# Two units instead of three in the first gated sweep, scores of two heads in turn into four banks, one normalising product per pair

## The chip, the cores and the metric

The kernel runs on one core of a Trainium2 chip. The metric is the device time of one execution in microseconds. The engines are TensorE (PE, with its weight loads PEld), VectorE (DVE), ScalarE (ACT), GpSimd (POOL) and SyncE (SP), whose queue starts nearly all DMA transfers.

## What is computed

```python
# attention, batch 2, 8 heads, 768 positions, head size 64; n_global = 8, n_local = 96
scores = q @ k.T / sqrt(64) - slope[h] * dist      # kept: first n_global keys, last n_local keys
a = softmax(scores); x = a @ v                     # x: 1536 rows of 512
# gated block, d_ff = 1536
xn = x / rms(x) * rms_g
y = (silu(xn @ w_gate) * (xn @ w_val)) @ w_out
# top-1 of 8 experts, 512 -> 1024 -> 512
out[mask_e] = gate_w[mask_e] * (relu(y[mask_e] @ w1[e]) @ w2[e])
```

## The kernel before

**Attention.** The 1536 rows are six stages of two tiles of 128 rows. For each stage the kernel goes through four pairs of heads, and a unit is one tile of rows of one pair: 6 x 4 x 2 = 48 units, numbered from 0. `scores` (L511) multiplies queries and keys of the two heads of a unit into two PSUM tiles `sp`; DVE adds the table of distances and takes the row's least value (L557, into `pr` and `mx`); ACT takes the exponential (L561). `turn` (L569) transposes the probabilities on PE (`pp`, L572), and ACT copies them to `ptS` (L580). `values` (L585) multiplies them by the values (`xp`, L601), and after the pair's second tile DVE takes the reciprocal of the sums (L608, L609) and writes the normalised rows into `duo` (L611), one product for each of the two tiles. A unit's turn is issued two units behind its scores, its values three more behind that.

The first eight pairs (units 0 to 15, `is_raw`, L203) multiply queries and keys as they are, in full fp32: head 0 lies on partitions 0 to 63, head 1 on 64 to 127, and each product contracts over 64 rows of the array (L533 in the first two tiles of a batch; later L537 for the 32 global keys and L538 for the others). The pairs after that split queries and keys into a high and a low fp32r part (ACT L486 and L498, DVE L499, POOL L489) and contract over all 128 rows (L550). All scores take their banks from the tag `s`, which has two. In units 0 to 15 `warm` (L176) issues two products of zeros behind a unit's scores, into banks of the tag `mm`, which has three.

**The gated block.** When a stage's rows are done, `tail` (L381) normalises them (ACT L387, DVE L393), transposes (L400) and splits them into `xn` (ACT L403, DVE L404). The 12 slices of d_ff (m = 0 to 11, called gated units here) are done in sweeps: a sweep takes a few gated units for all six stages, so that the weights in SBUF serve six times. `moe_block` (L762) is one stage of one sweep: 24 products of 256 columns per gated unit (`pg`, L769), tanh and the gating (ACT L777, DVE L778 and L782, ACT L786, POOL L787), and 6 output products of 512 columns per gated unit (`po`, L806), accumulated over the sweep's units. Sweep 0 has units 0 to 2, sweep 1 units 3 and 4, sweep 2 units 5 and 6, the last 7 to 11. Sweep 0 is issued between the attention's units, as far as a credit of 0.5 per unit allows (loop at L1163); the other sweeps and what is left follow the attention.

**The weights** come as float64. `prep_steps` (L361) gives three steps per gated unit (gate, value, output). A step loads 512 KB through one of three buffers `raw` (L322) and converts it in `convert64`: ACT L334, four DVE operations (L337, L340, L343, L346), ACT L353, and L354 for the low part, on POOL during the attention and on DVE behind it (`pin["sweep"]`). `PREPS` says at which unit the next step of sweep 0's weights is issued; those of later sweeps are issued between the blocks of the sweep ahead.

**What sets the order.** Each engine runs its instructions in the order in which they stand on it. That order is not the written one: the framework places instructions by its own estimate of when they are ready, written order giving the priority, so that work written later can stand ahead. Where the table `PREPS` or the split into sweeps changes, the places of many instructions change.

Of the kernel before, what the change touches and what calls it, by code (L numbers as in the profile page):

```python
# [45 lines left out]
def kernel(  # L46
# [23 lines left out]
    M0 = [3] * NSTAGE  # L70
    M1 = 7
    PM = [[0, 1, 2], [3, 4, 5, 6], [7, 8, 9], [10, 11]]
# [5 lines left out]
    PREPS = [2, 4, 6, 7, 11, 12, 20, 28, 36]  # L78
# [98 lines left out]
    def warm(n, after=None):  # L177
        for _ in range(n):
            w = psum.tile([P, 512], F32, tag="mm", bufs=NMM, name="warm")
            i = nc.tensor.matmul(  # L180
                out=w.rearrange("p (a n) -> p a n", a=4), lhsT=wz, rhs=wz.unsqueeze(1).to_broadcast([P, 4, P]),
                start=True, stop=True,
            )
            if after is not None:
                behind(i, after)

# [103 lines left out]
    def body(is_fast):  # L290
# [70 lines left out]
        def prep_steps(ms, pool, nslot):  # L361

            steps = []
            for m in ms:
                def gv(i, w, m=m):
                    if i == 0:
                        weights[m, 0] = pool.tile([P, 2, 2, KD, P], F32R, tag="gv", bufs=nslot, name=f"gv{m}")
# [4 lines left out]
                def ow(m=m):  # L372
                    t = weights[m, 1] = pool.tile([P, 2, DM], F32R, tag="ow", bufs=nslot, name=f"ow{m}")
# [3 lines left out]
                steps += [lambda gv=gv: gv(0, w_gate), lambda gv=gv: gv(1, w_val), ow]  # L377
            return steps
# [31 lines left out]
        def fast_attention(pool):  # L410
# [102 lines left out]
            def scores(g, t):  # L513
# [4 lines left out]
                else:  # L518
                    sp = [ps("s", NS, "sp") for _ in range(2)]
# [7 lines left out]
                if raw_:  # L527
                    kn, kgr_ = kt
                    for j in range(2):
                        r = slice(D * j, D * (j + 1))  # L530
                        lq = qt[r, t * P:(t + 1) * P]
                        if t0 == 0:
                            mm = nc.tensor.matmul(  # L533
                                out=sp[j][:, 0:n], lhsT=lq, rhs=kn[r, 0:n], start=True, stop=True
                            )
                        else:
                            nc.tensor.matmul(out=sp[j][:, 0:GW], lhsT=lq, rhs=kgr_[r, hp, :], start=True, stop=True)  # L537
                            mm = nc.tensor.matmul(  # L538
                                out=sp[j][:, GW:n], lhsT=lq, rhs=kn[r, t * P + GW:(t + 2) * P], start=True, stop=True
                            )  # L540
# [12 lines left out]
                un = units.index((g, t))  # L553
                if un < WARMU:
                    warm(WARM2[un % len(WARM2)], mm)
# [29 lines left out]
            def values(g, t, ptf, nb):  # L585
# [19 lines left out]
                if t == nt - 1:  # L605
# [4 lines left out]
                    for tt in range(nt):  # L610
                        nc.vector.tensor_tensor(  # L611
                            out=part[STARTS[st] + tt][:, hp * P:(hp + 1) * P].rearrange("p (j d) -> p j d", j=2),
                            in0=xp[:, tt * VW + 1:tt * VW + 1 + P].rearrange("p (j d) -> p j d", j=2),
                            in1=rc[:, tt].unsqueeze(2).to_broadcast([P, 2, D]), op=ALU.mult,
                        )
# [539 lines left out]
        preps = prep_steps(PM[0], wp, 3)  # L1155
# [9 lines left out]
        while True:  # L1165
# [9 lines left out]
            while preps and nun > PREPS[9 - len(preps)]:  # L1175
                preps.pop(0)()
            credit += MOE_RATE
            while True:
                if moe is None and ready:
                    st = ready.pop(0)  # L1180
                    moe = moe_block(0, range(M0[st]), st, mpool, False)
# [14 lines left out]
        nx = prep_steps(PM[1], ea, 4)  # L1196
# [14 lines left out]
        for st in ready:  # L1211
            run(moe_block(0, range(M0[st]), st, mpool, False))
        drain(f() for f in nx)
        for lo, hi, ms, pool, nslot, every in ((3, 5, PM[2], wp, 3, 4), (5, M1, PM[3], ea, 4, 5)):
            nx = prep_steps(ms, pool, nslot)
# [164 lines left out]
```

## Time and profile before

| | us |
|---|---|
| median of 3 runs | 655.6 (655.58 to 659.03) |
| the profiled execution | 655.69 |
| its span, first to last instruction | 654.0 |
| PE busy | 628.9 (96%) |
| DVE busy | 446.2 (68%) |
| ACT busy | 320.3 (49%) |
| POOL busy | 208.7 (32%) |

Times in the trace count from the span's start. The scores of unit 0 come at 8.5 us, the last product of the attention's values at 170 us; behind that stand the gated sweeps and the experts. A matmul's row in a timeline lasts until its result is in PSUM, so the next one starts ahead of its end, and what one costs PE is read from start to start.

### The profile page before, as it was taken

What the parts mean: (1) busy time and instruction counts of PE and PEld (TensorE: products, weight loads), DVE (VectorE), ACT (ScalarE), POOL (GpSimd) and SP (SyncE); (2) the same over time, 40 slices, a digit from 0 to 9 for tenths busy, and PEclk for the clock granted to TensorE, in tenths of its full rate; (3) what the DMA queues carried; (4) which work ended last, traced back from release to release, by engine and by line L of the source; (5) the groups of instructions that cost most, each with busy time, mean ns of one, the idle gap of its engine ahead of it and who ended that gap; (6) DMA issues with size and microseconds to landing.
All of it is one profiled execution on the core that took longest, in us unless ns stands there. A gap on an engine that the chain in (4) does not pass through costs nothing. (4 is left out here: it accounts for less than half of the span.)

```text
span 654.0 us, 11691 instructions
## 1 busy us (share of the span) xinstructions
PE 628.9 (96%) x4280; PEld 562.3 (86%) x4281; DVE 446.2 (68%) x1098; ACT 320.3 (49%) x624; POOL 208.7 (32%) x275
## 2 busy tenths in 40 slices
PE   9998998899999999999999999999999999999992
PEld 4667887899999999999999999997888899899891
DVE  5765888976599988676359998944667464664410
ACT  3666798777555533334622221333656564654420
POOL 4415758663122212111222532461610221011010
PEclk9999899899999999999999999999999999999997
DMA  7536466551044532131311010442978667454000
GB/s 228 158 90 201 127 174 181 157 149 39 1 130 130 161 98 72 59 98 65 129 65 65 2 65 34 122 138 82 301 261 261 206 217 253 168 189 140 17 13 30
DMA packets 56567, 82.98 MB, mean 127 GB/s; under 512 B 7983, under 2 KB 38703, under 8 KB 56496
## 3 DMA queue, kind: packets, MB, share of 16 engines
q1 hardware_dynamic: 53552, 74.75, 36.9%
q0 software_dynamic: 2944, 7.35, 3.4%
q8 instruction: 37, 0.61, 0.4%
q14 instruction: 34, 0.28, 0.1%
HBM read 75.75 MB, written 7.39 MB: 127 GB/s over the span
## 5 line engine op out<-in xcount | busy, mean ns | idle before, releaser
L769 PE MATMUL pg<-xn,gv 128*128 128x256 f32 x1728 | 228.2, 285 | 1.2 <-DVE th L778 1.2
L769 PEld LDWEIGHTS pg<-xn,gv 128*128 128x128 f32 x1728 | 220.2, 192 | 8.2 <-DVE th L778 1.5
L787 POOL TENSOR_TENSOR hid<-hf,hid 128x256 fp32r<-128x256 f32 x72 | 61.4, 855 | 174.6 <-ACT hid L786 174.5
L806 PE MATMUL po<-ow,hid 128*128 128x512 f32 x432 | 113.9, 394 | 0.0
L1017 PE MATMUL py<-ew,eh 128*128 128x512 f32 x384 | 91.2, 395 | 0.9 <-DVE eh L1084 0.5
L1017 PEld LDWEIGHTS py<-ew,eh 128*128 128x128 f32 x384 | 71.3, 188 | 17.7 <-DVE eh L1084 0.9
L806 PEld LDWEIGHTS po<-ow,hid 128*128 128x128 f32 x432 | 75.5, 189 | 11.7 <-POOL hid L787 0.3
L1039 PE MATMUL ph<-xs,ew 128*128 128x256 f32 x672 | 83.1, 283 | 0.0
L1039 PEld LDWEIGHTS ph<-xs,ew 128*128 128x128 f32 x672 | 81.6, 191 | 0.7
L786 ACT ACTIVATE hid<-hf 128x256 fp32r<-128x256 f32 x72 | 29.9, 417 | 83.7 <-DVE hf L782 81.9
L1024 POOL DMA_INDIRECT out_dram<-yo,tk x16 | 16.5, 1034 | 139.1 <-ACT yo L1023 107.7
L838 DVE CUSTOM_DVE_ANT_0 jk<-duo,rgb 128x512 bf16<-128x512 f32 x64 | 54.3, 849 | 0.5
L561 ACT ACTIVATE pr<-pr,mx 128x256 f32<-128x256 f32 (+1 forms) x96 | 45.1, 484 | 14.0 <-DVE mx L557 13.2
L957 DVE TENSOR_TENSOR ew<-rawe,ew 128x1024 fp32r<-128x1024 f32 (+1 forms) x36 | 40.8, 1134 | 12.9 <-ACT ew L953 12.9
L1048 DVE SCALAR_TENSOR_TENSOR eh<-ph,eh 128x256 fp32r<-128x256 f32 x56 | 23.1, 423 | 37.5 <-ACT eh L1047 35.5
L777 ACT ACTIVATE th<-pg 128x256 f32<-128x256 f32 x72 | 27.2, 379 | 39.8 <-PE pg L769 37.3
L957 DVE TENSOR_TENSOR ew<-duo,ew 128x1024 fp32r<-128x1024 f32 x28 | 34.1, 1224 | 17.9 <-ACT ew L953 16.8
L953 ACT ACTIVATE ew<-rawe 128x1024 fp32r<-128x1024 f32 x36 | 38.0, 1059 | 10.2 <-PE pg L769 4.6
L778 DVE SCALAR_TENSOR_TENSOR th<-th,pg 128x256 f32<-128x256 f32 x72 | 29.7, 415 | 16.4 <-ACT th L777 15.4
L1047 ACT ACTIVATE eh<-ph 128x256 fp32r<-128x256 f32 x56 | 21.2, 384 | 39.2 <-PE ph L1039 38.1
L953 ACT ACTIVATE ew<-duo 128x1024 fp32r<-128x1024 f32 x28 | 29.4, 1059 | 19.4 <-PE py L1017 19.4
L815 DVE TENSOR_TENSOR duo<-duo,po 128x512 f32<-128x512 f32 x36 | 23.4, 684 | 18.7 <-PE po L806 18.6
(178 smaller groups left out, 935.8 us busy)
## 6 DMA issues: line engine op xcount, KB each, us to landing
rawe<-in_moe_w_dram SPq DMA_DIRECT2D x36, 512.0 KB, 5.0
duo<-in_moe_w_dram SPq DMA_DIRECT2D x28, 512.0 KB, 5.4
raw<-in_moe_w_gate_dram SPq DMA_DIRECT2D x12, 512.0 KB, 3.8
raw<-in_moe_w_val_dram SPq DMA_DIRECT2D x12, 512.0 KB, 5.6
raw<-in_moe_w_out_dram SPq DMA_DIRECT2D x12, 512.0 KB, 3.4
kn<-in_k_dram SPq DMA_DIRECT2D x28, 192.0 KB, 3.3
qn<-in_q_dram SPq DMA_DIRECT2D x36, 128.0 KB, 2.9
vn<-in_v_dram SPq DMA_DIRECT2D x16, 192.0 KB, 2.6
```

Source lines behind the costliest of these rows:

```text
L561: pin["act"] = nc.scalar.activation(out=pr[:, j, 0:n], in_=pr[:, j, 0:n], func=ACTF.Exp, bias=mx[:, t, j:j + 1], scale=-1.0,)
L769: nc.tensor.matmul(out=pg[:, 0:n_], lhsT=gv[:, i, a, kk, :], rhs=x[st][:, kk, :], start=(n == 0), stop=(n == 3 * KD - 1),)
L777: pin["th"] = nc.scalar.activation(out=th, in_=pss[0][:, 0:n_], func=ACTF.Tanh, scale=0.5)
L778: nc.vector.scalar_tensor_tensor(out=th, in0=th, scalar=1.0, in1=pss[0][:, 0:n_], op0=ALU.add, op1=ALU.mult)
L786: nc.scalar.activation(out=hh[:, 0], in_=hf, func=ACTF.Copy)
L787: nc.gpsimd.tensor_tensor(out=hh[:, 1], in0=hf, in1=hh[:, 0].bitcast(F32), op=ALU.subtract)
L806: nc.tensor.matmul(out=po, lhsT=hid[mi][:, a, t * P:(t + 1) * P], rhs=ow[:, c, :], start=(mi == 0 and n == 0), stop=(mi == len(ms) - 1 and ...
L838: nc.vector.tensor_tensor_reduce(out=jk, in0=part[i0 + t], in1=rgb[e // 4][:, e % 4, :], scale=1.0, scalar=0.0, op0=ALU.mult, op1=ALU.add, ...
L953: cp = nc.scalar.activation(out=t[:, 0], in_=raw, func=ACTF.Copy)
L957: nc.vector.tensor_tensor(out=t[:, 1, 0:nd], in0=raw[:, 0:nd], in1=t[:, 0, 0:nd].bitcast(F32), op=ALU.subtract)
L1017: last_mm["py"] = nc.tensor.matmul(out=py, lhsT=hid(m, a, j), rhs=w2t[m // 2][:, c, (m % 2) * DM:(m % 2 + 1) * DM], start=(n == 0), stop=( ...
L1039: nc.tensor.matmul(out=ph[:, 0:CAP], lhsT=w1t[kk][:, a, m * P:(m + 1) * P], rhs=x[:, kk, :], start=(n == 0), stop=(n == 3 * KD - 1),)
```

## The change

- The sweeps have units 0 and 1, then 2 to 4, then 5 and 6, then 7 to 11. The number of products is the same. Weight steps of sweep 0 are six instead of nine; both output steps come last. Weights of units 0, 1, 2, 7, 8, 9 lie in one pool of three slots, the others in one of four that opens when the attention's buffers are free.
- Raw scores (units 0 to 15): the products of the two heads are issued in turn and held in that order. Units with an odd number take their banks from `mm`, so that four banks serve. The two products of zeros go ahead of the scores and into the same banks.
- One normalising product per pair writes both tiles.

```diff
-    M0 = [3] * NSTAGE
+    M0 = 2
-    PM = [[0, 1, 2], [3, 4, 5, 6], [7, 8, 9], [10, 11]]
+    PM = [[0, 1], [2, 3, 4], [5, 6, 7, 8], [9, 10, 11]]
-    PREPS = [2, 4, 6, 7, 11, 12, 20, 28, 36]
+    PREPS = [2, 4, 6, 8, 16, 20]
...
+        def slot(m):
+            return (wp, 3) if m in (0, 1, 2, 7, 8, 9) else (ea, 4)
...
-                steps += [lambda gv=gv: gv(0, w_gate), lambda gv=gv: gv(1, w_val), ow]
-            return steps
+                steps += [lambda gv=gv: gv(0, w_gate), lambda gv=gv: gv(1, w_val)]
+                (ows if ow_last else steps).append(ow)
+            return steps + ows
...
-                    sp = [ps("s", NS, "sp") for _ in range(2)]
+                    un = units.index((g, t))
+                    mmb = is_raw(st, hp) and un % 2
+                    sp = [ps(*(("mm", NMM) if mmb else ("s", NS)), "sp") for _ in range(2)]
...
-                    for j in range(2):
-                        r = slice(D * j, D * (j + 1))
-                        lq = qt[r, t * P:(t + 1) * P]
-                        if t0 == 0:
-                            mm = nc.tensor.matmul(
-                                out=sp[j][:, 0:n], lhsT=lq, rhs=kn[r, 0:n], start=True, stop=True
+                    mm = warm(WARM2[un % len(WARM2)], into=sp) if un < WARMU else None
+                    rows = [slice(D * j, D * (j + 1)) for j in range(2)]
+                    if t0 == 0:
+                        parts = [((0, n), kn[:, 0:n])]
+                    else:
+                        parts = [((0, GW), kgr_[:, hp, :]), ((GW, n), kn[:, t * P + GW:(t + 2) * P])]
+                    for (c0, c1), keys in parts:
+                        for o, r in zip(sp, rows):
+                            last_, mm = mm, nc.tensor.matmul(
+                                out=o[:, c0:c1], lhsT=qt[r, t * P:(t + 1) * P], rhs=keys[r], start=True, stop=True
                             )
+                            if last_ is not None:
+                                behind(mm, last_)
...
-                    for tt in range(nt):
-                        nc.vector.tensor_tensor(
-                            out=part[STARTS[st] + tt][:, hp * P:(hp + 1) * P].rearrange("p (j d) -> p j d", j=2),
-                            in0=xp[:, tt * VW + 1:tt * VW + 1 + P].rearrange("p (j d) -> p j d", j=2),
-                            in1=rc[:, tt].unsqueeze(2).to_broadcast([P, 2, D]), op=ALU.mult,
-                        )
+                    nc.vector.tensor_tensor(
+                        out=duo[st][:, :, hp * P:(hp + 1) * P].rearrange("p t (j d) -> p t j d", j=2),
+                        in0=xs3[:, :, 1:P + 1].rearrange("p t (j d) -> p t j d", j=2),
+                        in1=rc[:, 0:nt].unsqueeze(3).to_broadcast([P, nt, 2, D]), op=ALU.mult,
+                    )
...
-        for lo, hi, ms, pool, nslot, every in ((3, 5, PM[2], wp, 3, 4), (5, M1, PM[3], ea, 4, 5)):
-            nx = prep_steps(ms, pool, nslot)
+        for lo, hi, ms, every in ((M0, 5, PM[2], 4), (5, M1, PM[3], 4)):
+            nx = prep_steps(ms)
```

**How the order moves: scores on PE.** Units 10 to 12, raw scores. `sp` is the bank of a head's scores, `kgr` the 32 global keys, `kn` the others, `warm` or `sp<-wz` a product of zeros, `pp` a transpose. Before:

```order
L537 MATMUL sp<-kgr,qn 128x32
L538 MATMUL sp<-kn,qn 128x224
L572 MATMUL pp<-ident,pr 128x128 x2
L537 MATMUL sp<-kgr,qn 128x32
L538 MATMUL sp<-kn,qn 128x224
L180 LDWEIGHTS wz
L180 MATMUL warm<-wz 128x512
```

Now (L547 is the raw score, L580 the transpose):

```order
L181 LDWEIGHTS wz
L181 MATMUL sp<-wz 128x512
L547 MATMUL sp<-kgr,qn 128x32 x2
L547 MATMUL sp<-kn,qn 128x224 x2
L580 MATMUL pp<-ident,pr 128x128 x4
```

Before, transposes stood between the two heads of a unit; now the second head's product follows the first's, for the global keys and then for the others.

**Conversions on DVE.** Around units 20 to 22 (`pr,mx<-sp` is the score step of a head, `qt` a split of queries, `cv` a conversion step, `th` and `hf` the gating). Before:

```order
L393 SCALAR_TENSOR_TENSOR duo_114<-duo_114,ry,gB 128x512 x2
L778 SCALAR_TENSOR_TENSOR th<-th,pg 128x256
L557 ISA pr,mx<-sp,tabG 128x256
L557 ISA mx 128x1
L557 ISA pr,mx<-sp,half_170 128x256
L557 ISA mx 128x1
L608 TENSOR_SCALAR rc<-xp 128x4
L609 RECIPROCAL rc<-rc 128x4
L611 TENSOR_TENSOR duo_115<-xp,rc 128x128 x2
```

Now (L565 is the score step, L507 the split of queries, L339 to L348 the conversion, L785 the gating):

```order
L507 SCALAR_TENSOR_TENSOR qt<-qn,qt 128x2x256
L339 TENSOR_SCALAR cv<-cv 128x512
L342 TENSOR_SCALAR cv<-cv 128x512
L339 TENSOR_SCALAR cv<-cv 128x512
L785 SCALAR_TENSOR_TENSOR th<-th,pg 128x256
L565 ISA pr,mx<-sp,tabG 128x256
L565 ISA mx 128x1
L345 SCALAR_TENSOR_TENSOR cv<-raw,cv 128x512
L565 ISA pr,mx<-sp,half_170 128x256
```

Of the 11 conversions that stand among the attention's score steps on DVE, in both orders, 6 stood ahead of unit 16, 2 among units 16 to 29 and 3 among units 30 to 47; now it is 4, 7 and none. The three for gated unit 2 also do their low part on DVE (L356).

**Gated products on PE.** Around unit 42, late in the attention. Before (`pg` is a gate or value product, `po` an output product):

```order
L806 MATMUL po<-ow_1641,hid 128x512 x3
L769 MATMUL pg<-xn_246,gv_335 128x256 x13
L572 MATMUL pp<-ident,pr 128x128 x3
L550 MATMUL sp<-kt,qt 128x256 x4
L572 MATMUL pp<-ident,pr 128x128
L769 MATMUL pg<-xn_246,gv_335 128x256 x4
L572 MATMUL pp<-ident,pr 128x128 x4
```

Now (L561 is the split score, L408 the transpose of finished rows, L609 a value product):

```order
L561 MATMUL sp<-kt,qt 128x256 x4
L580 MATMUL pp<-ident,pr 128x128 x4
L561 MATMUL sp<-kt,qt 128x256 x2
L580 MATMUL pp<-ident,pr 128x128 x4
L561 MATMUL sp<-kt,qt 128x256 x2
L408 MATMUL trx<-ident,duo_116 128x128 x4
L609 MATMUL xp<-vx,ptS 128x65
```

From unit 39 to unit 47 no gated product stands between the scores any more. Up to the last value product of the attention PE had 216 `pg` and 39 `po`; now it has 147 and 30. Of these, 60 and none stood ahead of the scores of unit 30, where 85 and 12 stand now; between the scores of unit 30 and those of unit 47 132 and 30 stood before, 35 and 12 stand now. Ahead of the scores of unit 16 there were 48 turns' transposes and 44 value products; now there are 40 and 24.

## Rows read from the trace of the kernel before

**Rows 1.** The page: busy time, and PE's busy tenths in 40 slices.

```profile
PE 628.9 (96%) x4280; PEld 562.3 (86%) x4281; DVE 446.2 (68%) x1098; ACT 320.3 (49%) x624; POOL 208.7 (32%) x275
...
PE   9998998899999999999999999999999999999992
```

**Rows 2.** Windows: length, busy us (x) of PE, PEld, DVE, ACT, POOL; clock, DMA.

```profile
8.00:58.50 50.50, 49.91 (x292) 33.07 (x292) 34.18 (x123) 32.34 (x69) 21.52 (x37) 1.00 0.57 171
58.50:102.00 43.50, 38.48 (x296) 35.47 (x296) 35.75 (x120) 36.35 (x82) 26.26 (x39) 0.96 0.59 164
102.00:161.00 59.00, 55.40 (x433) 53.25 (x433) 47.23 (x143) 45.09 (x97) 38.93 (x57) 0.97 0.48 129
161.00:170.20 9.20, 9.20 (x76) 8.82 (x74) 3.50 (x12) 3.76 (x9) 1.34 (x4) 1.00 0.08 23
```

**Rows 3.** Waits of PE, 8 to 170 us: total us, times, longest; the largest one.

```profile
PE sp L550 <- DVE mx L557: 4.6, 7, 1.4
```

**Rows 4.** Timeline of PE: start, length, operation; raw scores and what follows them.

```profile
9.22 0.48 PE L533 MATMUL sp<-duo 64*128 64x128 f32 x2
9.64 0.60 PE L180 MATMUL warm<-wz 128*128 128x512 bf16 x2
10.17 0.70 PE L533 MATMUL sp<-duo 64*128 64x256 f32 x2
10.80 0.39 PE L180 MATMUL warm<-wz 128*128 128x512 bf16 x1
...
42.46 0.41 PE L537 MATMUL sp<-kgr,qn 64*128 64x32 f32 x2
...
43.26 0.61 PE L180 MATMUL warm<-wz 128*128 128x512 bf16 x2
...
56.07 0.42 PE L537 MATMUL sp<-kgr,qn 64*128 64x32 f32 x4
...
56.88 0.60 PE L180 MATMUL warm<-wz 128*128 128x512 bf16 x2
57.32 0.60 PE L572 MATMUL pp<-ident,pr 128*128 128x128 f32 x4
57.76 0.33 PE L601 MATMUL xp<-vx,ptS 128*128 128x65 f32 x2
...
58.15 0.39 PE L601 MATMUL xp<-vx,ptS 128*128 128x65 f32 x2
```

**Rows 5.** Timeline of ACT: the split of the keys of the tenth pair.

```profile
62.24 0.84 ACT L486 ACTIVATE kt<-kn 128x768 fp32r<-128x768 f32 x1 [2.43 <-DMA kn<-in_k_dram]
```

**Rows 6.** Groups of DVE, 8 to 166 us: busy, mean ns, idle before.

```profile
L343 DVE SCALAR_TENSOR_TENSOR cv<-raw,cv 128x512 uint32<-128x512 uint32 x11 | 9.8, 888 | 0.1
L346 DVE SCALAR_TENSOR_TENSOR cv<-raw,cv 128x512 uint32<-128x512 uint32 x11 | 9.2, 840 | 0.0
...
L337 DVE TENSOR_SCALAR cv<-cv 128x512 f32<-128x512 f32 x11 | 6.4, 580 | 2.4 <-ACT cv L334 2.4
L340 DVE TENSOR_SCALAR cv<-cv 128x512 uint32<-128x512 uint32 x11 | 6.4, 579 | 0.1
```

**Rows 7.** Window 84 to 101 us, then a group of PE and one of ACT there.

```profile
84.00:101.00 17.00, 15.85 (x127) 14.52 (x126) 14.95 (x64) 16.18 (x39) 10.25 (x16) 1.00 0.68 194
...
L769 PE MATMUL pg<-xn,gv 128*128 128x256 f32 x12 | 2.1, 299 | 0.0
...
L561 ACT ACTIVATE pr<-pr,mx 128x256 f32<-128x256 f32 (+1 forms) x14 | 6.2, 455 | 0.0
```

**Rows 8.** Window 206 to 300 us, then the groups of PE there.

```profile
206.00:300.00 94.00, 94.00 (x675) 88.13 (x675) 78.40 (x148) 37.51 (x79) 19.93 (x22) 1.00 0.32 100
...
L769 PE MATMUL pg<-xn,gv 128*128 128x256 f32 x537 | 69.3, 279 | 0.0
L806 PE MATMUL po<-ow,hid 128*128 128x512 f32 x138 | 38.5, 393 | 0.0
```

**Rows 9.** Groups of DVE, 170.2 to 206 us: a conversion's last step.

```profile
L346 DVE SCALAR_TENSOR_TENSOR cv<-raw,cv 128x512 uint32<-128x512 uint32 x8 | 6.5, 812 | 0.1
```

More of the change, by code (lines that the diff above doesn't have):

```diff
@@ L174, in behind, with warm @@
         )
-    def warm(n, after=None):
-        for _ in range(n):
-            w = psum.tile([P, 512], F32, tag="mm", bufs=NMM, name="warm")
+    def warm(n, after=None, into=None):
+        i = None
+        for k_ in range(n):
+            w = into[k_ % 2] if into else psum.tile([P, 512], F32, tag="mm", bufs=NMM, name="warm")
             i = nc.tensor.matmul(
@@ L185, in warm @@
                 behind(i, after)
+        return i
     qT = [q[b].rearrange("h d s -> (h d) s") for b in range(B)]
@@ L359, in body, with prep_steps @@
         pin = {"act": None, "dve": None, "th": None, "sweep": False}
-        def prep_steps(ms, pool, nslot):
-            steps = []
+        def slot(m):
+            return (wp, 3) if m in (0, 1, 2, 7, 8, 9) else (ea, 4)
+        def prep_steps(ms, ow_last=False):
+            steps, ows = [], []
             for m in ms:
                 def gv(i, w, m=m):
+                    pool, nslot = slot(m)
                     if i == 0:
@@ L372, in ow @@
                 def ow(m=m):
+                    pool, nslot = slot(m)
                     t = weights[m, 1] = pool.tile([P, 2, DM], F32R, tag="ow", bufs=nslot, name=f"ow{m}")
@@ L552, in scores @@
                     )
-                un = units.index((g, t))
-                if un < WARMU:
-                    warm(WARM2[un % len(WARM2)], mm)
                 for j in range(2):
@@ L1154, in body @@
         att = fast_attention(apool) if is_fast else dense_attention(apool)
-        preps = prep_steps(PM[0], wp, 3)
+        preps = prep_steps(PM[0], True)
+        npreps = len(preps)
         ready = []
@@ L1174, in body @@
                 late_loads()
-            while preps and nun > PREPS[9 - len(preps)]:
+            while preps and nun > PREPS[npreps - len(preps)]:
                 preps.pop(0)()
@@ L1180, in body @@
                     st = ready.pop(0)
-                    moe = moe_block(0, range(M0[st]), st, mpool, False)
+                    moe = moe_block(0, range(M0), st, mpool, False)
                     credit = 0.0
@@ L1195, in body @@
         ea = ea_cm.__enter__()
-        nx = prep_steps(PM[1], ea, 4)
+        nx = prep_steps(PM[1])
         yields = [0]
@@ L1211, in body @@
         for st in ready:
-            run(moe_block(0, range(M0[st]), st, mpool, False))
+            run(moe_block(0, range(M0), st, mpool, False))
         drain(f() for f in nx)
-        for lo, hi, ms, pool, nslot, every in ((3, 5, PM[2], wp, 3, 4), (5, M1, PM[3], ea, 4, 5)):
-            nx = prep_steps(ms, pool, nslot)
+        for lo, hi, ms, every in ((M0, 5, PM[2], 4), (5, M1, PM[3], 4)):
+            nx = prep_steps(ms)
             for st in range(NSTAGE):
```

5 lines of the change are left out of this document (removed).

## The prediction

> **What bounds the kernel now.** I read the page first: PE is busy for 96% of the span, and in its 40 slices the only ones under 9 lie among the first eight (about 130 us) and at the end [rows 1]. From 206 to 300 us PE has no idle time at all at the full granted clock [rows 8]; there only fewer products could save anything, and the change leaves their number as it is. So the question is when the attention ends on PE and how much gated work is then still to do. The windows cut the attention in four: units 0 to 15 (50.5 us), units 16 to 29 (43.5 us), units 30 to 47 (59.0 us) and a drain of 9.2 us up to 170.2 us [rows 2]. In the first PE is busy for 49.9 us of 50.5: it is the bound, though DVE and ACT have a third of their time free. In the second PE, ACT and DVE have 38.5, 36.4 and 35.8 us of work in 43.5 us, and no engine has much room. In the third PE is the bound again (55.4 of 59.0), since it has 132 `pg` and 30 `po` beside the attention. PE's largest wait is for DVE's score step, 4.6 us in seven pieces [rows 3].
>
> All that follows is summed against the profiled execution, 655.69 us with a span of 654.0, which is 0.1 us from the median of the runs.
>
> **Two heads in turn: less work on PE.** One head's raw scores hold PE for 0.42 us in the first tile (9.22 to 9.64), 0.63 us in the second (10.17 to 10.80), and 0.80 us in tiles with global keys (42.46 to 43.26) [rows 4]. In one unit, the last raw one, the two heads happen to stand next to each other already: eight matrix instructions from 56.07 to 56.88, 0.81 us, as long as one head's four [rows 4]. The two halves of the array work at the same time, in full fp32 too. The new order puts them together in all 16 units (in one, a product of zeros stands between the last two; I cost that at nothing). Four first tiles, four second ones and seven of eight with global keys save 4 x 0.42 + 4 x 0.63 + 7 x 0.80 = 9.8 us of PE. The products of zeros stay as many as they were. If the overlap failed in the new places, it would be 0.
>
> **First stretch, units 0 to 15.** In the new order 20 value products and 8 turns that stood ahead of unit 16's scores stand behind them, at 0.20 us (57.76 to 58.15 is two) and 0.11 us (57.32 to 57.76 is four) [rows 4], together 4.9 us that the second stretch gets back. PE is left with 49.9 - 9.8 - 4.9 = 35.2 us. DVE had 34.2 us here and loses two of six conversions. A conversion is 0.89 + 0.84 + 0.58 + 0.58 = 2.9 us [rows 6], so DVE has 28 us, and ACT no more than its 32.3. The four banks let a unit's scores start while DVE still reads those before. What is late next are the keys of the first split pairs: they need buffers that raw pairs hold until their scores are done, and ACT waited 2.4 us for those of the tenth pair before [rows 5]. I take 38 us, PE's work and one such stall (ends: 35, and 45 if loads pace it throughout).
>
> **Second stretch, units 16 to 29.** Seven conversions instead of two: 5 x 2.9 = 14.4 us more on DVE. It also gets three low parts that POOL had (one step of 128x512, nearest the last step of a conversion, 0.8 us: 2.4 us), the gating of about one more gated unit and a few normalising steps that come earlier (some 3 us, an estimate from the order's counts and steps of 0.6 to 0.9 us of that size). The merged normalising product saves the start of seven small ones, under 1 us. That makes 35.8 + 14.4 + 2.4 + 3 - 1 = 54.6 us of work on DVE, which becomes the bound. From 84 to 101 us the busiest engine, ACT, worked 16.2 of 17.0 us, 95% [rows 7]. At that share the stretch takes 57 us; the conversion's price may be lower where POOL rests (the 0.42 to 0.69 us of its best instances would make it 2.2 us, and the stretch 52 us). I take 56 (ends 50 and 62), 12.5 us longer than before.
>
> **Third stretch, units 30 to 47.** No conversion is left, and 97 `pg` and 18 `po` go. A gated product's price is read where nothing else runs: 537 `pg` of 256 columns and 138 `po` of 512 in 94 us [rows 8], with the second counted double 94 / 813 = 0.116 us, so 0.116 and 0.231. PE is left with 55.4 - 97 x 0.116 - 18 x 0.231 = 40.0 us. What the attention does with hardly any gated products is seen from 84 to 101 us: 14 exponentials of heads, seven units, in 17.0 us, with ACT at 95% and 12 `pg` beside them [rows 7]. 18 units at that pace take 43.7 us. I take 43.5 (ends 40, PE's own work, and 50), 15.5 us shorter. The drain stays 9.2.
>
> **What is put off.** Up to the attention's last value product PE has 69 `pg` and 9 `po` fewer. They come later, where PE has no idle time: 69 x 0.116 + 9 x 0.231 = 10.1 us. Behind the attention, 25 of the 36 conversions are left in both kernels. Now sweep 0 has 141 `pg` and 42 `po` to go, 26 us, and then sweep 1 needs gated units 2, 3 and 4; unit 2 is ready, unit 3 lacks one step and unit 4 all three. DVE finished eight in 35.8 us there [rows 9], so four take 18 us of 26. That cover is thin but holds; without it PE would wait for what is missing, at 4.5 us a step.
>
> **The sum.** The last value product comes at 8 + 38 + 56 + 43.5 + 9.2 = 154.7 us instead of 170.2, 15.5 us earlier; 10.1 us of that is given back. 655.7 - 5.4 = **650.3 us**. The same from PE's side: 9.8 us of work go, and idle time grows by 4.4.
>
> **A rule that speaks against it.** The third stretch leaves PE with transposes and short products. From 84 to 101 us PE had the same mixture, and the granted clock was 1.00, the level of 2.4 GHz [rows 7]; the lower shares, 0.96 and 0.97, belong to the stretches with PE's waits [rows 2]. The Trainium skill, TensorE: Matmul & The Clock Gate (Part 4, PE-mode transpose), says that transposes don't count as busy for the clock in the same way as products. By that rule the third stretch could fall to 1.2 GHz; the trace speaks against it for this mixture, and it is the last rival below.
>
> **Rivals.**
> 1. *Slower: DVE's conversions starve PE.* One mechanism, in units 16 to 29: conversions stand between the score steps in DVE's fixed order, PE has nothing else to do (its gated work needs the same DVE for the gating), and behind unit 30 there is no gated work left to fill with. Its price is the second stretch at 62 us and the third at 50, with 40 for the first: 8 + 40 + 62 + 50 + 9.2 = 169.2, and 10.1 us given back, 664.8 us. It decides from the point where the last value product is later than 160 us. For it: DVE's 54.6 us pass PE's own work there, 38.5 + 4.9 + 25 x 0.116 + 12 x 0.231 = 49 us by the order's counts. Against it: from 84 to 101 us ACT and DVE were busy for 95% and 88%, and PE still for 93% [rows 7]. Halfway lies 658.
> 2. *No change: loads pace the first stretch.* Each pair's keys wait for the buffer of the pair two ahead, so a faster PE meets a later DMA [rows 5]. At 44 us instead of 38 the sum is 656.3.
> 3. *The change doesn't do what it says:* the two heads do not overlap when the first of them follows products of zeros into the same banks. The first stretch is 45 us and more, 658 to 660. The instance at 56.07 speaks against it.
> 4. *Better than forecast:* conversions at 2.2 us and the third stretch at PE's own 40: 8 + 36 + 51 + 41 + 9.2 = 145.2, so 640.8.
> 5. *The clock falls* in the third stretch: PE's 40 us become 80, and 650.3 turns into 687.
>
> **How the numbers follow.** The forecast, within some 4 us, gets 0.50; rival 1 gets 0.20, half of it near its halfway point; rival 2 gets 0.13, rival 3 0.05, rival 4 0.10, rival 5 0.02. Two runs of this kernel can be told apart from no change by about 0.5%, 3.3 us, so faster means under 652.4. Most of the forecast (0.45) and rival 4 make 0.55 for faster; rival 2 and the edges of the forecast and of rival 1 make 0.20 for the same; the rest, 0.25, is slower. The range of 8 in 10 reaches most of the way to rival 4 and to 661, into rival 1: 643 to 661. The forecast's own range is 646 to 654.
>
> **What would show it.** In the profile after: raw scores of both heads as groups of four within 0.8 us in every unit; unit 16 at about 46 us; DVE busy for over 90% between units 16 and 29; the last value product near 155 us; and no idle time on PE from there to the experts. Wrong would be: pairs of heads that still take 1.6 us a unit, the last value product later than 160 us, or waits of PE for gated weights behind the attention.

## The result, and the profile after

The change made the kernel slower: 665.71 us (median of 4 runs, 663.25 to 668.63) against 655.59 (median of 4 runs of the kernel before beside them, 654.17 to 659.03), ratio 1.0135, 95% interval 1.0102 to 1.0168. The profiled execution took 663.25 us with a span of 661.6, 7.6 us more than the span before. That is 2.5 us under the median of the change, so the accounts below explain 7.6 of the 10.1 us between the medians.

The page after, busy time, PE in 40 slices, and the granted clock in tenths:

```profile
PE 627.3 (95%) x4280; PEld 561.7 (85%) x4281; DVE 443.5 (67%) x1077; ACT 318.5 (48%) x624; POOL 201.5 (30%) x272
...
PE   8896979889999999999999999999999999999991
...
PEclk9799979899999999999999999999999999999996
```

Six of PE's first nine slices are under 9, where three of eight were [rows 1], and the clock dips in three of the first eight. Windows of the change, with the columns of [rows 2]: units 0 to 15, 16 to 29, 30 to 47, the drain, all four, and the two that follow:

```profile
8.00:51.50 43.50, 40.07 (x262) 24.84 (x259) 25.86 (x102) 27.29 (x63) 15.89 (x29) 0.92 0.58 172
51.50:107.50 56.00, 47.77 (x345) 45.15 (x344) 47.72 (x136) 41.79 (x90) 29.66 (x43) 0.91 0.64 183
107.50:158.00 50.50, 44.74 (x348) 41.98 (x347) 38.77 (x125) 41.17 (x90) 31.91 (x54) 0.97 0.42 115
158.00:166.30 8.30, 8.30 (x70) 8.04 (x68) 3.20 (x8) 3.23 (x7) 2.37 (x5) 1.00 0.01 2
8.00:166.30 158.30, 140.88 (x1019) 120.01 (x1016) 115.56 (x368) 113.48 (x247) 79.82 (x131) 0.94 0.52 149
166.30:206.00 39.70, 39.70 (x290) 37.47 (x289) 30.62 (x62) 22.31 (x48) 8.70 (x10) 1.00 0.27 80
206.00:300.00 94.00, 94.00 (x670) 87.95 (x669) 73.64 (x137) 34.96 (x76) 19.81 (x22) 1.00 0.27 85
```

The same window of the kernel before, up to its last value product:

```profile
8.00:170.20 162.20, 152.99 (x1091) 130.61 (x1091) 120.65 (x394) 117.54 (x253) 88.05 (x136) 0.98 0.52 146
```

These two whole rows give an account that the rest of the text uses. A length splits into PE's **idle** time (length less busy), what the **lowered clock** cost (length times what the granted clock lacks of 1), and the **work** at full clock that is left. Before: 162.2 = 9.2 + 3.2 + 149.8. After: 158.3 = 17.4 + 9.5 + 131.4. The trace gives the clock to 0.01, so the clock and the work of an account are good to about 0.8 us. So 18.4 us of PE's work did leave the attention (the forecast's 9.8 and 10.1 make 19.9), but idle time grew by 8.2 us and the clock cost 6.3 more, and the last value product came only 3.9 us earlier. Behind it PE is busy all the time at clock 1.00 up to 300 us, as before [rows 8], with 495.3 us to go instead of 483.8. That is 11.5 us more, 10.1 of them put off, and 11.5 - 3.9 = 7.6.

PE's waits, 8 to 166 us (columns as in [rows 3]):

```profile
PE sp L561 <- DVE mx L565: 8.6, 8, 1.7
PE xp L609 <- DVE duo L618: 3.6, 4, 1.7
PE pp L580 <- ACT pr L569: 2.7, 1, 2.7
```

The wait for the score step has nearly doubled [rows 3]. The one for `duo` is new: it is for value banks that the merged product frees later, and e11, below, shows what taking it away is worth. The one for `pr` was 0.4 us before and lies in the first stretch. Timeline of ACT, then of PE, start, length, operation, idle time before:

```profile
13.25 0.38 ACT L588 ACTIVATE ptS<-pp 128x256 f32<-128x256 f32 x1 [1.17 <-PE pp L580]
20.04 0.42 ACT L459 ACTIVATE kg<-kgn 128x256 fp32r<-128x256 f32 x1 [6.41 <-DMA kgn<-in_k_dram]
20.36 1.48 ACT L569 ACTIVATE pr<-pr,mx 128x256 f32<-128x256 f32 x4
```

```profile
17.73 0.49 PE L547 MATMUL sp<-duo 64*128 64x128 f32 x4
20.91 0.69 PE L580 MATMUL pp<-ident,pr 128*128 128x128 f32 x2 [2.68 <-ACT pr L569]
...
30.01 0.41 PE L547 MATMUL sp<-kgr,qn 64*128 64x32 f32 x4
30.25 0.63 PE L547 MATMUL sp<-kn,qn 64*128 64x224 f32 x4
30.81 0.44 PE L580 MATMUL pp<-ident,pr 128*128 128x128 f32 x2
```

ACT's order has a copy of the global keys (L459) ahead of the first units' exponentials. Its input lands late, ACT stands for 6.4 us, and PE runs dry. Before, ACT stood 2.6 us for the same copy (at 19.5 us), and PE was busy for 49.9 of the stretch's 50.5 us [rows 2]. From 20.91 two transposes take 0.69 us that take 0.44 at 30.81, where the clock is back. Windows of the change around it, PE well fed, after the wait, and later:

```profile
12.00:17.70 5.70, 5.51 (x31) 2.60 (x30) 1.49 (x9) 0.46 (x2) 1.61 (x5) 1.00 1.08 360
20.20:26.80 6.60, 5.89 (x20) 2.95 (x21) 3.93 (x14) 5.93 (x15) 1.61 (x4) 0.50 0.11 19
27.00:40.00 13.00, 12.90 (x98) 8.87 (x97) 12.28 (x40) 9.10 (x21) 4.78 (x5) 1.00 0.51 154
```

After the wait the granted clock was 0.50, the lower level (1.2 GHz), with PE busy for 89% of the window. The two heads' scores do overlap: 30.01 to 30.81 is 0.80 us for eight instructions, which one head took before [rows 4].

### The profile page after: what moved, and what is told of

It is laid out like the page before. It is cut to its first block, busy times and chain, and to the rows that moved or that the text cites. A ratio compares the mean times of both kernels' runs of the same rounds, so it can differ in the third digit from the quotient of the medians.

```text
span 661.6 us, 11642 instructions
## 1 busy us (share of the span) xinstructions
PE 627.3 (95%) x4280; PEld 561.7 (85%) x4281; DVE 443.5 (67%) x1077; ACT 318.5 (48%) x624; POOL 201.5 (30%) x272
## 5 line engine op out<-in xcount | busy, mean ns | idle before, releaser
L1031 POOL DMA_INDIRECT out_dram<-yo,tk x16 | 16.5, 1031 | 138.0 <-ACT yo L1030 107.6
L569 ACT ACTIVATE pr<-pr,mx 128x256 f32<-128x256 f32 (+1 forms) x96 | 43.1, 482 | 11.2 <-DVE mx L565 11.0
L785 DVE SCALAR_TENSOR_TENSOR th<-th,pg 128x256 f32<-128x256 f32 x72 | 29.7, 414 | 20.6 <-ACT th L784 19.4
L561 PE MATMUL sp<-kt,qt 128*128 128x256 f32 (+1 forms) x128 | 27.5, 314 | 9.6 <-DVE mx L565 8.6
```

The source lines that it names most:

```text
L561: mm = nc.tensor.matmul(out=o, lhsT=qt[:, j, a, t * P:(t + 1) * P], rhs=rhs, start=(a == 0), stop=(a == 1))
L569: pin["act"] = nc.scalar.activation(out=pr[:, j, 0:n], in_=pr[:, j, 0:n], func=ACTF.Exp, bias=mx[:, t, j:j + 1], scale=-1.0,)
L785: nc.vector.scalar_tensor_tensor(out=th, in0=th, scalar=1.0, in1=pss[0][:, 0:n_], op0=ALU.add, op1=ALU.mult)
```

## The experiments

Each account is of the profiled execution, from 8 us to the last value product; the last column is what is left of the span. The time of that one execution stands beside the median, since it can lie some us from it. The ratios stand against the kernel before on the same chip, and are not quotients of the medians shown.

| run | median us | profiled | ratio, 95% interval | length | idle | clock | work | after it |
|---|---|---|---|---|---|---|---|---|
| before | 655.6 | 655.7 | | 162.2 | 9.2 | 3.2 | 149.8 | 483.8 |
| the change | 665.7 | 663.3 | 1.0135, 1.0102 to 1.0168 | 158.3 | 17.4 | 9.5 | 131.4 | 495.3 |
| e1 scores alone | 657.8 | 657.1 | 1.0034, 1.0013 to 1.0054 | 163.4 | 15.8 | 8.2 | 139.4 | 484.0 |
| e2 sweeps alone | 667.4 | 667.9 | 1.0156, 1.0113 to 1.0199 | 161.7 | 14.6 | 8.1 | 139.0 | 496.2 |
| e8 merged product alone | 662.0 | 661.4 | 1.0093, 1.0063 to 1.0122 | 166.5 | 11.7 | 6.7 | 148.1 | 485.2 |
| e14 copy held alone | 669.0 | 665.1 | 1.0189, 1.0150 to 1.0228 | 175.6 | 13.4 | 5.3 | 156.9 | 479.8 |
| e9 scores, copy held | 655.2 | 653.3 | 0.9996, 0.9971 to 1.0020 | 159.5 | 13.2 | 6.4 | 139.9 | 484.1 |
| e4 scores, merged product, copy held | 654.9 | 656.4 | 0.9980, 0.9946 to 1.0014 | 161.6 | 11.2 | 9.7 | 140.7 | 485.1 |
| e7 the same, zeros at unit 16 | 657.6 | 654.4 | 1.0008, 0.9989 to 1.0027 | 158.3 | 10.4 | 6.3 | 141.6 | 486.4 |
| e3 change, copy held | 661.2 | 661.2 | 1.0073, 1.0043 to 1.0103 | 156.4 | 14.6 | 12.5 | 129.3 | 495.1 |
| e5 e3, conversions spread | 666.0 | 666.4 | 1.0162, 1.0098 to 1.0225 | 162.6 | 14.0 | 19.5 | 129.1 | 494.2 |
| e6 e5, credit 0.7 | 658.2 | 658.6 | 1.0032, 1.0008 to 1.0057 | 159.4 | 14.6 | 6.4 | 138.4 | 489.5 |
| e10 sweeps alone, credit 0.7 | 661.7 | 660.4 | 1.0086, 1.0049 to 1.0124 | 164.8 | 13.2 | 3.3 | 148.3 | 485.5 |
| e11 e3, two products | 668.1 | 670.1 | 1.0164, 1.0129 to 1.0199 | 166.3 | 18.1 | 18.3 | 129.9 | 494.0 |
| e12 e11, credit 0.7 | 672.5 | 674.1 | 1.0204, 1.0160 to 1.0248 | 175.4 | 16.0 | 19.3 | 140.1 | 488.9 |
| e13 e3, credit 0.7 | 657.6 | 654.0 | 1.0014, 0.9991 to 1.0037 | 155.5 | 11.5 | 4.7 | 139.3 | 488.8 |
| e15 e3, credit 0.6 | 656.1 | 660.1 | 0.9986, 0.9963 to 1.0008 | 159.5 | 10.3 | 11.2 | 138.0 | 490.9 |
| e16 e3, credit 0.8 | 656.5 | 658.1 | 1.0004, 0.9980 to 1.0027 | 162.2 | 11.2 | 13.0 | 138.0 | 486.2 |

### The parts alone

**e1**, the raw scores on the kernel before:

```diff
-                    for j in range(2):
-                        r = slice(D * j, D * (j + 1))
+                    for (c0, c1), keys in parts:
+                        for o, r in zip(sp, rows):
```

> The kernel before with the raw scores of the change alone (heads in turn, four banks, products of zeros ahead); three units in the first sweep and two normalising products as before. Its order keeps conversions and gated products of units 16 to 47 as before (4 + 2 of the conversions ahead of unit 16, 216 gate products up to the last value product), but ACT's copy of the global keys stands ahead of unit 1's exponentials, as in the change. Theory A (the sweeps and the conversions they gather in units 16 to 29 cost the time; the scores gain): units 0 to 15 some 7 us shorter, the rest as before, 647 to 650 us. Rival B (the scores' new order itself costs the time, by the stall at the start and the lower clock behind it): 655 us or more.

**e2**, the sweeps alone:

```diff
-    M0 = [3] * NSTAGE
+    M0 = 2
-    PREPS = [2, 4, 6, 7, 11, 12, 20, 28, 36]
+    PREPS = [2, 4, 6, 8, 16, 20]
```

> The change's sweeps and weight steps alone, with the scores and products of the kernel before. Seven of 11 conversions still stand among units 18 to 31.5 on DVE, and 120 gate products ahead of unit 47's scores. Theory A: all of the loss without the scores' gain, units 16 to 29 over 10 us longer than before, 663 to 672 us. Rival B: within 2 us of the kernel before, 654 to 658 us.

**e8**, the merged product alone:

```diff
-                    for tt in range(nt):
-                        nc.vector.tensor_tensor(
+                    nc.vector.tensor_tensor(
```

> The kernel before with the merged normalising product alone. It saves 24 short DVE operations, some 0.15 us each by start to start, 3.6 us of DVE of which little is on the path: 653 to 656 us. If the merged product holds the one bank of the value products longer than the first of two did, and PE waits for it as in the change (3.6 us): 656 to 660 us.

Measured: 657.8, 667.4 and 662.0 us: e1 came out with its rival, e2 with its theory A, e8 above both of its ranges. The whole window of e1, then of e2:

```profile
8.00:171.40 163.40, 147.58 (x1092) 128.05 (x1091) 120.60 (x395) 115.35 (x253) 88.98 (x136) 0.95 0.51 144
```

```profile
8.00:169.70 161.70, 147.12 (x1020) 124.61 (x1018) 116.18 (x392) 113.94 (x247) 83.29 (x131) 0.95 0.51 146
```

The scores took 10.4 us of work off PE, close to the 9.8 of the forecast, and all of it came back, 6.6 us as idle time and 5.0 by the clock. Here too the copy stood ahead of the first units' exponentials, and ACT waited 7.59 us for it. The sweeps moved 10.8 us of work behind the attention, and the attention ended 0.5 us earlier for it. The merged product, by the forecast a saving of under 1 us on DVE, cost 6 us. The three costs, 1.8, 11.4 and 5.6 us between medians, add to 18.8, where the change lost 10.1: the parts don't add, so the loss can't be shared out by them.

### The copy of the global keys

**e3**, the change with the copy behind unit 6's exponentials:

```diff
-                if gi == 2:
-                    nc.scalar.activation(out=kg, in_=kgn, func=ACTF.Copy)
+                if gi == 4:
+                    behind(nc.scalar.activation(out=kg, in_=kgn, func=ACTF.Copy), pin["act"])
```

> The change with one instruction moved: ACT's copy of the global keys is held behind the exponentials of unit 6. Theory C (part of the loss is that ACT waits 6.4 us for those keys ahead of unit 1's exponentials, and PE then runs at the lower clock until about 27 us): units 0 to 15 some 4 to 6 us shorter than in the change, no stall of PE at 21 us; the time 3 to 6 us under the change, 658 to 662 us. Rival D (the first stretch is paced by loads of keys, or what it gains is lost to DVE in units 16 to 29): within 2 us of the change.

Measured: 661.2 us. Units 0 to 15, 16 to 29, 30 to 47:

```profile
8.00:45.70 37.70, 36.60 (x257) 23.17 (x255) 26.27 (x101) 27.25 (x62) 17.43 (x29) 1.00 0.67 196
45.70:102.10 56.40, 50.32 (x342) 47.26 (x341) 49.76 (x135) 41.65 (x89) 29.57 (x44) 0.85 0.63 182
102.10:155.90 53.80, 46.37 (x351) 43.84 (x350) 39.62 (x125) 41.33 (x91) 32.13 (x54) 0.94 0.41 108
```

The first stretch takes 37.7 us at clock 1.00, where the change had 43.5 at 0.92. That is 5.8 us, of which some 4 reach the median. The third got longer by 3.3.

**e4**, scores, merged product and the copy held, on the kernel before; **e9**, the same with the two products:

```diff
-                if gi == 2:
+                if gi == 4:
...
-                        r = slice(D * j, D * (j + 1))
+                        for o, r in zip(sp, rows):
```

> The kernel before with the raw scores of the change, one normalising product per pair, and the copy of the global keys held behind unit 6; three units in the first sweep. If theories A and C hold, 12 us less in units 0 to 15 and nothing lost behind: 642 to 647 us. If the merged product costs PE its waits for the one bank of value products (3.6 us in the change), 646 to 650. If loads pace units 0 to 15 whatever ACT does, 648 to 650.

> The kernel before with the raw scores of the change (heads in turn, four banks, zero products ahead only) and with ACT's copy of the global keys held behind unit 6's exponentials; the two normalising products per pair stay. Theory: of a stretch's time the engine PE pays its work at full clock, its idle time, and half of what it runs at half clock; the scores take 9.8 us of work away, and what gave it back in the run of scores alone (657.8) was the late copy (6.4 us of ACT's wait) and 10 us more at half clock. Held, and without the merged product that cost 5.6 us by itself: 649 to 652, the first 16 units by 46 us. Rival: the merged product's 5.6 us is chance of the order in that one kernel, and is not to be had here: 654 to 657, as the run with the merged product (654.9).

Measured: 654.9 and 655.2 us, both not to be told from before. The first lies outside all three of its ranges (642 to 650 together); the second was expected at 649 to 652 and came out with its rival. PE's work is 9 to 10 us less than before in both; 8.5 and 7.2 us of idle time and clock took its place. Where, is seen in e9, units 0 to 15, 16 to 29, 30 to 47:

```profile
8.00:48.48 40.48, 36.56 (x256) 23.42 (x256) 31.99 (x115) 29.92 (x67) 19.12 (x30) 1.00 0.72 215
48.48:93.95 45.47, 41.44 (x317) 39.10 (x315) 35.12 (x126) 35.58 (x80) 28.75 (x46) 0.92 0.53 150
93.95:158.46 64.51, 59.25 (x449) 56.19 (x449) 50.79 (x145) 45.69 (x100) 41.44 (x56) 0.95 0.44 122
```

The first stretch is 10.0 us shorter than before [rows 2], the scores' whole gain, and the second and third are 2.0 and 5.5 us longer. Why these two give it back is not shown.

**e7**, e4 with twelve products of zeros ahead of unit 16, where PE had stood idle for 2.5 us and then ran at the lower level:

```diff
+                if un == 16:
+                    fl = warm(12)
```

> e4_scores_prod_kg with 12 more products of zeros (2.6 us of PE) between the scores of units 15 and 16, where PE was idle for 2.5 us there and then ran for 6.8 us at the lower clock. Theory E (what the scores save is lost to the clock that falls behind such gaps): no low clock around 52 us, units 16 to 29 shorter by 3 us or more, the time 650 to 653 us. Rival G (units 16 to 29 are paced by DVE, ACT and POOL, whatever the clock): the clock stays up, but the time is within 1.5 us of e4_scores_prod_kg (654.9).

Measured: 657.6 us. Units 16 to 29 in e7:

```profile
48.80:93.70 44.90, 42.18 (x330) 38.71 (x329) 35.52 (x116) 35.26 (x81) 28.17 (x47) 0.96 0.53 149
```

The second stretch fell from 50.6 us at clock 0.83 to 44.9 at 0.96, as theory E wanted, but the third went from 58.2 to 63.3, and the median is no better: the time follows neither of the two.

### Conversions, and gated work beside the attention

**e5**, e3 with the five conversions that the change brings forward held behind units 30, 33, 36, 39 and 42:

```diff
+                    if every == 1 and 2 * pin["at"] < len(pin.get("all", ())):
+                        pin["act"] = pin["all"][2 * pin["at"] + 1]
+                    pin["at"] += 3
```

> The change with the copy of the global keys held behind unit 6 (as e3_after_kg) and the five conversions of the second sweep's weights that stood among units 21 to 29 held behind the exponentials of units 30, 33, 36, 39 and 42, so that units 16 to 29 have two conversions and units 30 to 47 five. Theory A (gathered conversions make DVE the bound of units 16 to 29, which took 56 us): that stretch falls to 44 to 48 us, the next grows by 0 to 5 us, and the time is 652 to 657 us, where e3_after_kg has 661. Rival F (not their place but the gated products that were put off and the lower clock cost the time): units 16 to 29 stay above 52 us and the time within 3 us of e3_after_kg.

Measured: 666.0 us. Units 16 to 29 in e5:

```profile
47.10:102.20 55.10, 50.19 (x355) 48.31 (x354) 36.10 (x119) 39.43 (x88) 28.80 (x46) 0.85 0.50 142
```

With two conversions there instead of seven, DVE's work fell from 49.8 to 36.1 us, and the stretch from 56.4 to 55.1. So DVE's conversions don't set its length; 4.9 us are PE's idle time and 8.3 the clock's. The third stretch, which now holds five of them, grew from 53.8 to 58.9 us, and the time is 4.8 us above that of e3, which neither theory had.

**e6**, the same with a credit of 0.7 a unit for gated products:

```diff
-    MOE_RATE = 0.5
+    MOE_RATE = 0.7
```

> e5_after_kg_spread with a credit of 0.7 instead of 0.5 per unit, so that 168 gate and 36 output products stand ahead of unit 47's scores instead of 120 and 24. If PE's idle time can take gated products (part of the loss is the filler that is lacking), 3 to 6 us less than e5_after_kg_spread. If PE waits for DVE's score steps and more gating on DVE lengthens these waits as much as the products save, within 2 us of it.

The same line gave **e10** (on e2), **e13** (on e3), and, with 0.6 and 0.8, **e15** and **e16** (on e3).

> The kernel before with the change's sweeps alone and the credit for gated products raised from 0.5 to 0.7, so that 208 instead of 151 gate and value products are issued before the last value product of the attention. The sweeps alone took 667.4. Theory that the sweeps cost because the attention has too few gated products to fill PE (idle time, and half clock after it): 657 to 661, with the low clock at most 15 us where it was 17 and the rest after the attention 6 us shorter. Rival, that the sweeps cost because their conversions are issued together (seven in units 16 to 29) or because the second sweep's slots are late: 665 or more, since the credit moves no conversion.

> The change with the copy of the global keys held (661.2 by itself) and the credit for gated products at 0.7, nothing else: 195 gate and 40 value products are issued before the attention's last value product, where 147 and 30 were. Theory that the missing products cost their own time after the attention (48 x 0.116 + 10 x 0.231 = 7.9 us) while in it they fill time in which PE was idle or slow: 653 to 657, the rest after the attention shorter by 6 to 8 us, the attention longer by no more than 4. Rival, which the run with two normalising products and 0.7 (672.5) speaks for: the third stretch is bound by another engine's order, the products stand in its way, and the attention grows by as much as the rest shrinks: 661 or more.

> The change with the copy of the global keys held and the credit at 0.6: 192 gate and 36 value products before the last value product, between the runs with 0.5 (147 and 30; 661.2) and 0.7 (195 and 40; 657.6). If cover is the reason, and not a lucky order at 0.7: 656 to 660. If the gain at 0.7 was luck of its order: 661 or more, as the run with two normalising products and 0.7 went.

> The same with the credit at 0.8: 192 gate and 48 value products. By cover 655 to 659; by luck of the order anything above 661.

Measured: 658.2, 661.7, 657.6, 656.1 and 656.5 us. "Cover" means that gated products fill time in which PE would otherwise idle or run slow. e15 and e16 lie where cover puts them, e10 and e13 less than a microsecond above, and e6 gained 7.8 us, where 3 to 6 were expected. Units 0 to 15, 16 to 29, 30 to 47 of e13:

```profile
8.00:46.70 38.70, 37.18 (x258) 23.39 (x257) 26.79 (x102) 27.26 (x63) 17.18 (x29) 1.00 0.64 191
46.70:99.10 52.40, 47.06 (x343) 44.70 (x342) 47.34 (x135) 41.50 (x90) 30.74 (x43) 0.90 0.65 187
99.10:154.20 55.10, 51.45 (x409) 48.09 (x408) 41.19 (x129) 43.54 (x96) 32.45 (x56) 1.00 0.41 111
```

The third stretch holds 58 more matrix instructions than in e3, takes 1.3 us longer, and its clock is 1.00 instead of 0.94. The work put in is counted in the traces, up to the last value product, at 0.116 us a `pg` and 0.231 a `po`; the other columns are of the table of accounts:

| pair | work put into the attention | attention longer by | after it shorter by | medians |
|---|---|---|---|---|
| e2 to e10 | 8.9 | 3.1 | 10.7 | -5.7 |
| e5 to e6 | 5.6 | -3.2 | 4.7 | -7.8 |
| e3 to e13 | 7.9 | -0.9 | 6.3 | -3.6 |
| e3 to e15 | 6.6 | 3.1 | 4.2 | -5.1 |
| e3 to e16 | 9.4 | 5.8 | 8.9 | -4.6 |
| e11 to e12 | 8.2 | 9.1 | 5.1 | +4.4 |

In five of six pairs, 6 to 9 us of gated products beside the attention lengthen it by 6 at most, and in two it is even shorter; most of the work is done in time that was idle or lost to the clock. The profiled execution of e13 lies 3.6 us under its median and that of e15 4.0 above, which shifts their rows by as much. Each pair also changes the order of many instructions, and no pair changes the products alone. With the copy held and the credit raised, the change is level with the kernel before, in three different orders.

### What an order is worth

**e11**, e3 with two normalising products per pair, and **e12**, that with credit 0.7:

```diff
-                    nc.vector.tensor_tensor(
+                    for tt in range(nt):
+                        nc.vector.tensor_tensor(
```

> The change with the copy of the global keys held (661.2) and with two normalising products per pair as before. If the merged product costs by itself what it cost in the kernel before (5.6 us), here too: 655 to 657, and the waits of PE for a value bank behind the product (3.6 us in the change) gone. If its cost there came with that kernel's order alone: 660 to 662.

> The same with the credit at 0.7 (207 gate and value products before the last value product). Theory of the missing products: 5 to 8 us less than with 0.5, so 649 to 652 if the two products give their 5.6 us and 653 to 656 if they don't; half clock in at most 15 us of the attention, the rest after it about 490. Rival, that the clock and the idle time don't follow the products: within 2 us of the run with 0.5.

Measured: 668.1 and 672.5 us; neither theory's numbers held, though PE's wait behind the product, from 45 to 160 us, was down from 2.5 us in e3 to 0.7 in e11. e12 is the one pair in which more products didn't pay, and why isn't settled. The merged product cost 6 us in the kernel before (e8), nothing beside the scores (e4 against e9), and saved 7 us in the change (e3 against e11). No price of its own is seen; what differs between these runs is the order in which the planner puts everything else.

**e14** is the control, the kernel before with only the copy held, the edit of e3 (POOL's step on the same keys is issued later with it), so that no engine's work changes.

> The kernel before with only ACT's copy of the global keys held behind unit 6's exponentials: no work is added or removed on any engine, but the planner's order shifts with it (239 instead of 216 gate products before the attention's last value product). A control for what a shifted order alone is worth. If orders that differ by chance are worth little: 654 to 658. If they are worth what the merged product seemed to cost (5.6 us) or gain: outside 651 to 661. The 23 products put ahead would give 2.7 us if they are covered, so 653 by the theory of cover.

Measured: 669.0 us, 12 us slower. Its whole window:

```profile
8.00:183.60 175.60, 162.21 (x1120) 136.81 (x1119) 124.08 (x395) 117.54 (x253) 90.24 (x137) 0.97 0.47 134
```

The profiled span is 9.4 us longer. 3.8 us are products put ahead (23 x 0.116 + 5 x 0.231), which come off the time behind it (4.0), 4.2 are idle time, 2.1 the clock; 3.3 us more of PE's busy time are no added products. No instruction waited for the held copy.

## Why the prediction was wrong

**The scores: right.** 9.8 us of work were forecast to go, 10.4 went (e1), with both heads' products in 0.80 us.

**First stretch: forecast 5.5 us too low, for one thing left out.** 38 us were forecast; the change took 43.5, and e3, without the copy in the way, 37.7. The forecast named ACT's waits for keys of later pairs [rows 5], but left out that ACT's own order had moved a copy whose input comes late ahead of unit 1's exponentials.

**Second stretch: the number right, its reason wrong.** 56 us were forecast and 56.0 measured. But DVE had 47.7 us of work there, not 54.6. Groups of DVE in the change, 51.5 to 107.5 us:

```profile
L345 DVE SCALAR_TENSOR_TENSOR cv<-raw,cv 128x512 uint32<-128x512 uint32 x7 | 5.9, 843 | 0.0
L348 DVE SCALAR_TENSOR_TENSOR cv<-raw,cv 128x512 uint32<-128x512 uint32 x7 | 5.6, 806 | 0.0
...
L342 DVE TENSOR_SCALAR cv<-cv 128x512 uint32<-128x512 uint32 x7 | 3.3, 467 | 0.1
L339 DVE TENSOR_SCALAR cv<-cv 128x512 f32<-128x512 f32 x7 | 2.9, 416 | 0.7 <-ACT cv L336 0.7
```

A conversion took 2.5 us, not 2.9 [rows 6], and e5 shows that taking five away shortens the stretch by 1.3 us. Its 56 us are 42.7 of PE's work, 8.2 idle and 5.0 by the clock. Two mistakes cancelled, by luck.

**Third stretch: the step that failed.** "18 units at that pace take 43.7 us", with the pace read from 84 to 101 us [rows 7]; it took 50.5, and 53.8 in e3. PE's work was 43.2 us (44.74 less the clock's 1.5), 3.2 more than the 40.0 forecast, and 5.8 us idle and 1.5 of clock came to it, where the forecast left 3.5 for both. No engine was bound: DVE had 38.8 us and ACT 41.2 of 50.5. PE's waits from 84 to 101 us before, then the two largest of the third stretch now:

```profile
PE sp L550 <- DVE mx L557: 0.7, 2, 0.5
...
PE sp L561 <- DVE mx L565: 4.3, 5, 1.7
PE xp L609 <- DVE duo L618: 1.3, 1, 1.3
```

The gated products that the third stretch still holds:

```profile
L776 PE MATMUL pg<-xn,gv 128*128 128x256 f32 x33 | 5.7, 303 | 0.0
L813 PE MATMUL po<-ow,hid 128*128 128x512 f32 x10 | 3.2, 416 | 0.0
```

One good window was taken for the pace of 18 units. It did not owe its pace to its gated products: 12 `pg` in 17.0 us [rows 7] are no more for their time than these in 50.5. It is the good part of its own stretch, which took 43.5 us for 14 units [rows 2], 3.1 us a unit, where the window has 2.4 and the third stretch now 2.8. PE waited for the score step in all of them; what sets that wait in the third stretch is not shown.

The counts behind these terms were also off by a unit: in the traces 96 `pg` and 17 `po` stand ahead of the scores of unit 30 now, not 85 and 12 (those stand ahead of the last score of unit 29), and 16, not 20, value products moved behind unit 16's scores. By the forecast's own prices that moves 2.4 us from the third stretch to the second and 0.8 us back to the first; what is put off stays 10.1.

**What is put off: its size right, its cover wrong.** The 10.1 us did come back (11.5). But the forecast let the third stretch shrink by all of the same work, to "PE's own 40". e2 shows the put-off work leaving and the attention only 0.5 us shorter, and the pairs of the second table speak for the reason: beside the attention that work filled time in which PE otherwise idles or runs slow. The line "9.8 us of work go, and idle time grows by 4.4" is where the sum fell: idle time grew by 8.2 and the clock cost 6.3 more, 10.1 us above what that line allowed. Another 1.5 is work that didn't leave (18.4 of 19.9), and 1.4 came after the attention; together 13.0, from -5.4 to +7.6. By stretches the same 13.0 are 5.5 in the first, none in the second, 7.0 in the third, 0.9 less in the drain, and 1.4 after the attention.

**The signs named ahead.** Both heads' scores did come within 0.80 us where the clock was up, and PE has no idle time from the last value product to 300 us. But unit 16 came at 50.4 us and not at 46 (44.9 in e3), DVE was busy for 85% between units 16 and 29 and not for over 90%, and the last value product came at 166.3, behind the 160 that was to be a sign of being wrong.

**The rivals.** Rival 1's number, 664.8, is near the 665.7 measured, and its second half, no gated work left to fill with behind unit 30, is half true: 33 `pg` and 10 `po` were left in the third stretch, none of them between the scores of units 39 and 47. Its mechanism, DVE's conversions in units 16 to 29, fell with e5. Rival 2, the loads, got a place in another form: one late load, in front of one copy. Rival 3 fell with the timeline, and rival 4's 2.2 us a conversion were 2.5. Rival 5's fall of the clock cost 1.5 us in the third stretch, not 40. The rule on transposes is neither shown nor excluded: the clock was lower in stretches with transposes and short products (0.97 in the third stretch of the change, 0.94 in that of e3, 1.00 in that of e13), but idle time lay in them too (5.8, 7.4 and 3.7 us), and no run separates the two.

**The cause, as far as it is shown.** Of the three parts the sweeps cost most (e2), and more gated products beside the attention gave 5.7 of their 11 us back (e10). The late copy cost the change some 4 us (e3), and the first stretch, where it stood, shows it. With the copy held and cover given back, nothing of the loss is left (e13, e15, e16), and no gain either: the scores' 10 us come in the first stretch and don't shorten the whole attention by more than 4 in any run on the kernel before with the copy held (e4, e7, e9). No version ran faster than the kernel before beyond its interval. What stays open is how much of each difference is its order's chance, which by e14 can be 12 us, more than the whole loss. So lost cover is the reading that fits five pairs of six, and not a cause that is shown.

## What to carry to other kernels

In these runs, work beside a stretch in which no engine is full mostly cost little there, and its full price once it was put off, so the price of moving it is read from both places. Before the pace of a good window is taken for a whole stretch, hold it against the mean of the stretch that it was cut from, and see in the order of every engine which late input now stands ahead of what. Where a planner sets the order, an edit that changes no work should be timed as a control before effects of its size are believed.

## What had not been expected of the hardware

The granted clock is a term of the sum here. In the ten runs of e4 the time goes with the clock, from 651.22 us at a mean of 0.985 to 659.80 at 0.972: 8.6 us, and 0.013 of a span of 655 us is 8.5. The tie is loose: two of the ten at 0.976 lie 3.0 us apart. After a gap of 2.7 us PE ran at 0.50 though it was busy again, and two transposes took 0.69 us for 0.44.
